# Masks by ScalarE and GpSimd, spatial weights in six pieces, and two pieces of work a unit later in a fused attention and MLP kernel

## The chip, the core and the metric

One core of a Trainium2 chip runs the whole program as one launch. The core has TensorE (PE; its weight loads are shown as PEld), VectorE (DVE), ScalarE (ACT), GpSimd (POOL), and SyncE (SP), which here issues every transfer. The metric is the device time of one execution in microseconds (us); smaller is better. Each engine works through its own list of instructions in order and waits at an instruction whose inputs or buffers aren't ready.

## The reference

Three stages for 4 batches of 768 tokens, the output of each being the input of the next.

```python
for t in range(S):                       # attention: 8 heads of 48, D = 48
    state = alpha[:, :, t, :, None] * state + einsum('bhd,bhe->bhde', k[:, :, t], v[:, :, t])
    y[:, :, t] = einsum('bhd,bhde->bhe', q[:, :, t], state)
x = y with the heads side by side        # 384 wide
xn = (x - mean) / sqrt(var + 1e-6) * g_ln
x = x + relu(xn @ w_ch1) @ w_ch2         # first MLP, 1536 wide
h = gelu(x @ w_in)                       # second MLP, 1024 wide
u, v = h[..., :512], h[..., 512:]
v_n = (v - mean) / sqrt(var + 1e-6) * g_ln
gated = u * (einsum('ts,bsd->btd', w_sg, v_n) + b_sg[None, :, None])   # mixes the 768 tokens of a batch
out = x + gated @ w_out
```

## The kernel before

**Precision.** Matmuls of the MLPs run in float16 with each operand split into a high half (rounded) and a low half (what rounding lost); three passes (high x high, low x high, high x low) make one product. So each weight and each intermediate result is followed by a ScalarE copy (high) and a subtraction (low) on VectorE or GpSimd. The helper `low` (L155) writes a low half on VectorE if its first argument is true, otherwise on GpSimd; `split2` (L151) does high and low with a scale, the low one on VectorE.

**Attention.** The 24 chunks of 128 tokens (6 a batch) each go through some 20 steps (`att_steps`): alpha is transposed, running products of it along the chunk (scans) give F and K, q and k are multiplied on, TensorE makes the scores of two sets of heads (tile sc in PSUM), the part above the diagonal is set to zero, and the masked scores times v plus q times the state give the output; its mean is taken off, its halves (xsp) are transposed by a transfer into xhT. For the first batch (chunks 0 to 5, `whole`) the scores stay float32 and `masked` makes the mask on VectorE in one instruction from PSUM (L499), by a product with the tile causal; for the later chunks masking goes other ways, which the change doesn't touch. From chunk 8 on, alpha, q and k are transposed by transfers instead of TensorE (L299, L302, L315). Input tiles inp are two; the load of chunk i + 2 waits for the last reading of chunk i (L565, `stats`).

**The MLPs.** Chunks go in 12 groups of two. For each group there are units of TensorE work: A (first product, L706, output hT by ScalarE L711 and VectorE L712), T (transposes of x), C (L787 gives v, then L816 gives u, both through gelu), B (second product, L740). For each batch there are six units D, the spatial mix (L837), and six units E, the output product (L866). In C, v is normalized: VectorE takes mean and variance (L792, L794), GpSimd makes the factor r2 in six instructions on single columns (`rms_scale`, L247 to L252), VectorE applies it (L799), and the halves vn follow (L802, `low`). This last part, `normalize`, is put off in the source: `finish` runs it while the next unit of C is written down. In D, VectorE scales the sum out of PSUM into one of two buffers tm (L843), GpSimd multiplies by u (L846), ScalarE writes the gate's high half (L847), GpSimd its low half (L848). Sums of TensorE rotate through three PSUM banks (tag g).

**Weights.** They are loaded, converted and split in pieces while the first batch runs, one step of `wstep` after the other; a step also issues the next load. Loads go into three tiles stage. The spatial weights w_sg (768 x 768) come in three pieces of two row blocks (`wg_piece`, L210); each row block is split into two halves wsp, of which there is one pair of buffers at a time (tag cv, shared with small scratch tiles), and each half is transposed by a transfer into wgs, which D reads.

**Order.** The kernel writes down units, attention steps, loads and weight steps in the order of due times that it works out by hand from the constants of L20 (`events`, L1011 on); the weight steps of the last kind are due from C3 = 60 at a distance of R3. The framework then places the instructions on each engine with a planner of its own, which estimates when each would be ready; what is written down first isn't always placed first. `tc.issue_after(x)` pins what is written inside it behind x on x's engine, in the order of issue alone.

## Time and profile before

| what | value |
|---|---|
| time, median of 3 runs | 695.94 us (693.63 to 696.15) |
| the profiled execution: its own time | 695.21 us |
| its span, first to last instruction | 693.4 us |
| mean granted TensorE clock | 0.978 of full speed |
| busy: PE, DVE, ACT, POOL | 640.0, 460.7, 376.4, 250.5 us |

A row's time is that of one profiled execution. The "chain that ended last" follows the work back from the last instruction, at each step to what it had waited for. Idle time of an engine costs nothing unless something later on the chain waits for it.

### The profile page before, as it was taken

Reading aid. Unit: us, or ns where it says so; the run is one execution under the profiler, and the core shown is the slowest. Engines: PE = TensorE matmul, PEld = TensorE weight load, DVE = VectorE, ACT = ScalarE, POOL = GpSimd, SP = SyncE. Lnnn points to the kernel's source line nnn. Section 1 sums busy time; section 2 is a strip of 40 time slices with the busy share of each in tenths; the row PEclk is TensorE's granted clock in tenths of the full one; section 3 lists DMA queues with packets and bytes.
Section 4 is the critical chain, followed back from the end, with each engine's and each line's share of the span. In section 5 each row is a group of like instructions: output and inputs, shape, how many; then the busy total and the mean of one; then the engine's idle time right before and its main releaser. Section 6 shows DMA issues by size and latency. Waiting matters only on the chain.

```text
span 693.4 us, 14269 instructions
## 1 busy us (share of the span) xinstructions
PE 640.0 (92%) x5622; PEld 487.4 (70%) x5622; DVE 460.7 (66%) x879; ACT 376.4 (54%) x643; POOL 250.5 (36%) x474
## 2 busy tenths in 40 slices
PE   5989798899999988999999989997989999999996
PEld 3677596676666875677686876675677887676783
DVE  7799977868655568667664669638966777333325
ACT  3765435487834576477844587646753733332230
POOL 4232220534423662342523770521415652302261
PEclk9999989999999998999999998999999999999999
DMA  9996889648824747764724638674523322110102
GB/s 226 280 243 183 252 169 182 102 81 122 115 29 71 104 62 125 142 111 91 107 50 60 103 67 170 104 115 76 89 44 68 76 26 58 28 19 12 36 1 74
DMA packets 228636, 70.63 MB, mean 102 GB/s; under 512 B 219472, under 2 KB 222544, under 8 KB 228560
## 3 DMA queue, kind: packets, MB, share of 16 engines
q1 hardware_dynamic: 228560, 69.63, 54.3%
q8 instruction: 46, 0.75, 0.5%
q14 instruction: 30, 0.25, 0.1%
HBM read 35.79 MB, written 4.72 MB: 58 GB/s over the span
## 4 chain that ended last, share of the span: by engine, by line
PE 51%; DVE 19%; DMA 12%; ACT 10%; issue 5%; POOL 2%; SPq 1%; ACTq 0%; DVEq 0%
PE pg L740 11%; PE pg L706 10%; PE pgs L837 10%; PE pgo L866 6%; PE pgu L816 4%; PE pgv L787 4%; ACT stage L315 3%; DMA xhT<-xsp 3%; DMA wgs<-wsp 3%; DMA stage<-stage 2%; DMA stage<-in_moe_w_ch_dram 2%; DVE st_in L565 2%; DVE F L362 2%; ACT stage L299 2%; DVE hT L712 2%
## 5 line engine op out<-in xcount | busy, mean ns | idle before, releaser
L706 PE MATMUL pg<-xhT,w1s 128*128 128x256 f16 (+1 forms) x1404 | 153.8, 270 | 14.6 <-DVE hT L712 12.5
L706 PEld LDWEIGHTS <-w1s 128*128 128x128 f16 x1404 | 131.1, 100 | 33.2 <-issue 16.1
L740 PE MATMUL pg<-w2s,hT 128*128 128x384 f16 x864 | 145.3, 326 | 0.4 <-DVE hT L712 0.4
L740 PEld LDWEIGHTS <-hT 128*128 128x128 f16 x864 | 83.6, 98 | 53.9 <-issue 0.6
L837 PE MATMUL pgs<-wgs,vn 128*128 128x256 f16 x864 | 96.0, 273 | 0.0
L837 PEld LDWEIGHTS <-vn 128*128 128x128 f16 x864 | 84.1, 98 | 10.3
L315 ACT ACTIVATE stage<-stage 128x1024 uint16<-128x1024 uint16 x48 | 64.2, 1350 | 9.3 <-DMA stage<-stage 9.2
L712 DVE SCALAR_TENSOR_TENSOR hT<-pg,hT 128x512 f16<-128x512 f32 (+1 forms) x74 | 48.7, 670 | 29.4 <-ACT hT L711 29.2
L299 ACT ACTIVATE stage<-inp 128x1024 uint16<-128x1024 uint16 x48 | 49.1, 1046 | 20.6 <-DVE K L362 10.6
L156 POOL TENSOR_TENSOR kh<-K,kh 128x512 f16<-128x512 f32 x17 | 21.6, 1268 | 105.5 <-ACT kh L469 105.5
L711 ACT ACTIVATE hT<-pg 128x512 f16<-128x512 f32 (+1 forms) x74 | 41.4, 575 | 31.2 <-PE pg L706 31.2
L816 PE MATMUL pgu<-x2T,wis 128*128 128x256 f16 x432 | 49.6, 273 | 3.2 <-ACT vg L790 1.4
L787 PE MATMUL pgv<-wis,x2T 128*128 128x512 f16 x216 | 49.2, 379 | 0.5 <-DVE hT L712 0.5
L816 PEld LDWEIGHTS <-wis 128*128 128x128 f16 x432 | 41.8, 98 | 9.9 <-issue 2.3
L866 PE MATMUL pgo<-wos,uT 128*128 128x384 f16 x288 | 48.3, 326 | 0.0
L156 POOL TENSOR_TENSOR qs<-F,qs 128x512 f16<-128x512 f32 x18 | 20.2, 1123 | 70.9 <-ACT qs L447 70.8
L866 PEld LDWEIGHTS <-uT 128*128 128x128 f16 x288 | 27.9, 98 | 17.8
L843 DVE SCALAR_TENSOR_TENSOR tm<-pgs,g2c,bbc 128x256 f32<-128x256 f32 x48 | 20.7, 474 | 28.2 <-PE pgs L837 22.9
L552 DVE SCALAR_TENSOR_TENSOR vs<-inp,vs 128x384 f16<-128x384 f32 x18 | 15.0, 833 | 32.9 <-ACT vs L550 32.9
L787 PEld LDWEIGHTS <-x2T 128*128 128x128 f16 x216 | 20.6, 98 | 22.9 <-issue 0.6
L247 POOL TENSOR_SCALAR ve<-mvv 128x1 f32<-128x1 f32 x24 | 5.6, 235 | 84.1 <-DVE mvv L794 83.0
L847 ACT ACTIVATE uT<-tm 128x512 f16<-128x512 f32 x24 | 15.0, 625 | 38.7 <-POOL tm L846 38.7
(184 smaller groups left out, 1108.8 us busy)
## 6 DMA issues: line engine op xcount, KB each, us to landing
stage<-in_moe_w_ch_dram SPq DMA_DIRECT2D x24, 384.0 KB, 5.3
inp<-in_alpha_dram SPq DMA_DIRECT2D x24, 192.0 KB, 4.6
inp<-in_q_dram SPq DMA_DIRECT2D x24, 192.0 KB, 3.4
inp<-in_k_dram SPq DMA_DIRECT2D x24, 192.0 KB, 4.1
inp<-in_v_dram SPq DMA_DIRECT2D x24, 192.0 KB, 4.5
out_dram<-x SPq DMA_DIRECT2D x24, 192.0 KB, 1.9
stage<-in_moe_w_in_dram SPq DMA_DIRECT2D x4, 768.0 KB, 4.7
stage<-in_moe_w_sg_dram SPq DMA_DIRECT2D x6, 384.0 KB, 4.2
```

Of the source, the lines that this page charges most:

```text
L156: (nc.vector if on_dve else nc.gpsimd).tensor_tensor(out=out, in0=in0, in1=in1, op=ALU.subtract)
L299: nc.scalar.activation(out=sp, in_=t[:, n].rearrange("p h d -> p (h d)").bitcast(U16) .rearrange("p (x w) -> p w x", w=2), func=AF.Copy)
L315: nc.scalar.activation(out=words[:, :, :, gap:], in_=tr, func=AF.Copy)
L706: nc.tensor.matmul(out=pg[:, f, :], lhsT=w1s[:, a, kk, ff * P:(ff + 1) * P], rhs=xhT[j][:, r, kk, o], start=(n_ == 0), stop=(n_ == 3 * KD ...
L711: nc.scalar.activation(out=hi, in_=src, func=AF.Relu)
L712: last_dve[0] = nc.vector.scalar_tensor_tensor(out=lo, in0=src, scalar=0.0, in1=hi, op0=ALU.max, op1=ALU.subtract)
L740: nc.tensor.matmul(out=box[s], lhsT=hidden(a, f, s), rhs=w2s[:, r, f, :], start=(f == 0 and a == 0 and r == 0), stop=(f == KF - 1 and r == 1))
L787: nc.tensor.matmul(out=pg, lhsT=x2T[j][:, a, kk, o], rhs=wis[:, r, kk, DG:DI], start=(n_ == 0), stop=(n_ == 3 * KD - 1))
L816: nc.tensor.matmul(out=pg[:, f, :], lhsT=wis[:, a, kk, ff * P:(ff + 1) * P], rhs=x2T[j][:, r, kk, 0:N], start=(n_ == 0), stop=(n_ == 3 * K ...
L837: nc.tensor.matmul(out=pg[:, f, :], lhsT=vn[b * NCH + s][:, a, d * P:(d + 1) * P], rhs=wgs[th][:, r, s, :], start=(n_ == 0), stop=(n_ == 3 ...
L843: nc.vector.scalar_tensor_tensor(out=tm[:, f, :], in0=pg[:, f, :], scalar=g2c[:, d:d + 1], in1=bbc[:, th * U:(th + 1) * U], op0=ALU.mult, ...
L866: nc.tensor.matmul(out=pg, lhsT=gt[key][:, d // 2, a, d % 2, o], rhs=wos[:, r, d, :], start=(d == 0 and a == 0 and r == 0), stop=(d == KG ...
```

## The change

Four edits and a constant.

- Masks of the first batch: ScalarE copies the scores out of PSUM with the scale, and GpSimd sets the part above the diagonal to zero in place (`affine_select`), instead of one VectorE instruction per set of heads; two sets for each of six chunks.
- Spatial weights: six pieces of one row block, each in a tile stage of its own, instead of three of two. ScalarE scales the block in place, ScalarE writes the high half, GpSimd subtracts for the low half. The distance R3 of the weight steps goes from 5 to 3, and the counts NW of steps that D and E need grow by three.
- Gate: high and low half (and, in the last batch, a square for a check) are written down a unit later, in the next unit of D, or in the next unit of A after a batch's last; `low` now puts every second low half on VectorE. `in_order` pins them behind the last instruction written on ScalarE, VectorE and GpSimd.
- v's normalization keeps its place in the source, but `in_order` pins it behind the last instruction written on ScalarE and VectorE.

```diff
--- before.py
+++ after.py
@@ -70,7 +70,7 @@
     NG3 = S // U
 
     NW = [KF // 2, KF, KF + DI // U]
-    NW += [NW[2] + NCH // 2, NW[2] + NCH // 2 + KG // 2]
+    NW += [NW[2] + NCH, NW[2] + NCH + KG // 2]
     NST = 3
     NF = NCH
 
@@ -208,18 +208,20 @@
     wo_piece = row_pieces(wos, w_out, S_WO, False)
 
     def wg_piece(i):
+
         if i == 0:
             wg_tiles()
-        t = stage_tile().bitcast(F32).rearrange("p (n s) -> p n s", n=2)
-        for n in range(2):
-            nc.sync.dma_start(out=t[:, n], in_=w_sg[(2 * i + n) * P:(2 * i + n + 1) * P, :])
+        t = stage_tile().bitcast(F32)[:, 0:S]
+        nc.sync.dma_start(out=t, in_=w_sg[i * P:(i + 1) * P, :])
 
         def split():
-            for n in range(2):
-                sp = [p2.tile([P, S], F16, tag="cv", name="wsp") for _ in range(2)]
-                split2(sp[0], sp[1], t[:, n], S_SG)
-                for a in range(2):
-                    nc.sync.dma_start_transpose(out=wgs[i][:, a, :, n * P:(n + 1) * P], in_=sp[a])
+            sp = [p2.tile([P, S], F16, tag="cv", name="wsp") for _ in range(2)]
+            nc.scalar.activation(out=t, in_=t, func=AF.Copy, scale=S_SG)
+            nc.scalar.activation(out=sp[0], in_=t, func=AF.Copy)
+            nc.gpsimd.tensor_tensor(out=sp[1], in0=t, in1=sp[0], op=ALU.subtract)
+            o = slice(i % 2 * P, i % 2 * P + P)
+            for a in range(2):
+                nc.sync.dma_start_transpose(out=wgs[i // 2][:, a, :, o], in_=sp[a])
         return split
 
     wgs = []
@@ -496,8 +498,9 @@
             if whole:
                 m = T[f"ss{e}"] = T[f"ss{e}"].rearrange("p a n t -> p (a n t)").bitcast(F32) \
                     .rearrange("p (n t) -> p n t", n=NP)
-                nc.vector.scalar_tensor_tensor(out=m, in0=T["sc", e], scalar=S_V, op0=ALU.mult, op1=ALU.mult,
-                                               in1=causal.unsqueeze(1).to_broadcast([P, NP, P]))
+                nc.scalar.activation(out=m, in_=T["sc", e], func=AF.Copy, scale=S_V)
+                nc.gpsimd.affine_select(out=m, in_=m, pattern=[[0, NP], [1, P]], compare_op=ALU.is_ge, fill=0.0,
+                                        base=0, channel_multiplier=-1)
                 return
             if chosen(MB):
                 m = T["sm", e] = T["sc", e]
@@ -678,6 +681,15 @@
     s_split = [None]
 
     last_dve = [None]
+
+    def in_order(work, *engines):
+
+        traced = nc.cur_bb.bb.instructions
+        with ExitStack() as behind:
+            for e in engines:
+                behind.enter_context(tc.issue_after(next(n for n in reversed(traced) if n.engine == e.engine)))
+            work()
+
     stats_step = {}
 
 
@@ -711,6 +723,7 @@
                     nc.scalar.activation(out=hi, in_=src, func=AF.Relu)
                     last_dve[0] = nc.vector.scalar_tensor_tensor(out=lo, in0=src, scalar=0.0, in1=hi, op0=ALU.max,
                                                                  op1=ALU.subtract)
+                    finish_gate()
                 units.append((unit, per * 9 * N / 2400.0, (2, 3, 5, 6)[((u + 1) * per - 1) // KD],
                               groups[j][0] * NCH + groups[j][1] + (part if j == 0 else 1)))
         return units
@@ -775,7 +788,7 @@
         def finish():
 
             if pending:
-                pending.pop()()
+                in_order(pending.pop(), nc.scalar, nc.vector)
 
         for s in range(n):
             i = b * NCH + c + s
@@ -822,6 +835,13 @@
             units.append((unit, per * 9 * N / 2400.0, NW[1] + KG // 2 + u + 1))
         return units
 
+    gate_pending = []
+
+    def finish_gate():
+
+        if gate_pending:
+            in_order(gate_pending.pop(0), nc.scalar, nc.vector, nc.gpsimd)
+
     def D_units(b):
         units = []
         for th in range(S // U):
@@ -844,12 +864,18 @@
                                                        in1=bbc[:, th * U:(th + 1) * U], op0=ALU.mult, op1=ALU.add)
                     o = slice(2 * dp, 2 * dp + 2)
                     nc.gpsimd.tensor_tensor(out=tm, in0=tm, in1=uT[key][:, o, :], op=ALU.mult)
-                    nc.scalar.activation(out=gt[key][:, dp, 0], in_=tm, func=AF.Copy)
-                    nc.gpsimd.tensor_tensor(out=gt[key][:, dp, 1], in0=tm, in1=gt[key][:, dp, 0], op=ALU.subtract)
-                    if b == B - 1:
-                        n_ = 2 * th + dp
-                        nc.scalar.activation(out=junk()[:, 0:512].rearrange("p (a b) -> p a b", a=2), in_=tm,
-                                             func=AF.Square, accum_out=st_g[:, n_:n_ + 1])
+                    finish_gate()
+
+                    def halves_of_gate():
+                        nc.scalar.activation(out=gt[key][:, dp, 0], in_=tm, func=AF.Copy)
+                        low(dp, gt[key][:, dp, 1], tm, gt[key][:, dp, 0])
+                        if b == B - 1:
+                            n_ = 2 * th + dp
+                            nc.scalar.activation(out=junk()[:, 0:512].rearrange("p (a b) -> p a b", a=2), in_=tm,
+                                                 func=AF.Square, accum_out=st_g[:, n_:n_ + 1])
+                    gate_pending.append(halves_of_gate)
+                    if b == B - 1 and th == S // U - 1 and dp == KG // 2 - 1:
+                        finish_gate()
                 units.append((unit, 36 * U / 2400.0, NW[3]))
         return units
 
@@ -940,7 +966,7 @@
                                     op0=ALU.mult)
         nc.vector.tensor_scalar(out=diags[0][:, KD], in0=ident, scalar1=S_W2, scalar2=None, op0=ALU.mult)
         pre = [(w1_piece, n) for n in range(KF // 2)] + [(w2_piece, n) for n in range(KF // 2)] \
-            + [(wi_piece, n) for n in (2, 3, 0, 1)] + [(wg_piece, n) for n in range(NCH // 2)] \
+            + [(wi_piece, n) for n in (2, 3, 0, 1)] + [(wg_piece, n) for n in range(NCH)] \
             + [(wo_piece, n) for n in range(KG // 2)]
         pre.reverse()
         ready = []
```

## Rows read from the trace of the kernel before

**Rows 1.** The page's fourth part: the chain of work that ended last, as shares of the span by engine.

```profile
PE 51%; DVE 19%; DMA 12%; ACT 10%; issue 5%; POOL 2%; SPq 1%; ACTq 0%; DVEq 0%
```

**Rows 2.** Busy time by stretch. Columns: start and end of the stretch, its length, busy time (and number of instructions) of PE, PEld, DVE, ACT and POOL, the granted TensorE clock, the transfers' share of the 16 DMA engines, and GB/s.

```profile
30.00:60.00 30.00, 27.20 (x324) 24.14 (x323) 27.02 (x47) 17.79 (x29) 9.98 (x19) 1.00 1.03 234
60.00:90.00 30.00, 24.50 (x188) 18.22 (x188) 28.66 (x50) 16.56 (x25) 5.42 (x14) 0.89 0.80 216
...
300.00:400.00 100.00, 99.50 (x925) 76.61 (x923) 62.76 (x116) 63.34 (x111) 45.66 (x80) 1.00 0.55 89
```

**Rows 3.** TensorE in order of time, around the first MLP of groups 0 and 1. Columns: start and duration in us, engine, line, operation, output and inputs, shapes, how many; in brackets the idle time of the engine just before and what ended it.

```profile
40.62 1.67 PE L706 MATMUL pg<-xhT,w1s 128*128 128x128 f16 x27 [1.02 <-DMA xhT<-xsp]
...
93.76 2.13 PE L706 MATMUL pg<-xhT,w1s 128*128 128x256 f16 x18
...
105.29 0.63 PE L460 MATMUL pk<-ident,K 128*128 128x128 f32 x4 [1.12 <-DVE K L320]
...
111.22 1.13 PE L577 MATMUL psd<-inp,ks 128*128 128x96 f32 x8 [1.45 <-ACT ks L461]
...
114.42 1.76 PE L604 MATMUL psy<-inp,ss 128*128 128x48 f32 x14 [0.55 <-DVE ss L499]
...
125.19 2.12 PE L816 MATMUL pgu<-x2T,wis 128*128 128x256 f16 x18 [0.76 <-DVE nmu L656]
```

**Rows 4.** VectorE (first five rows) and ScalarE (last row) in order of time, in the stretch of the masks and the spatial weights. Columns as in rows 3.

```profile
73.04 1.28 DVE L499 SCALAR_TENSOR_TENSOR wk<-sc,causal 128x512 f32<-128x512 f32 x2
...
87.41 0.61 DVE L659 SCALAR_TENSOR_TENSOR xsp<-psy,st_mv,xsp 128x384 f16<-128x384 f32 x1
...
99.59 0.96 DVE L153 SCALAR_TENSOR_TENSOR wsp<-stage,wsp 128x768 f16<-128x768 f32 x1 [3.13 <-DMA wgs<-wsp]
...
112.80 0.96 DVE L153 SCALAR_TENSOR_TENSOR wsp<-stage,wsp 128x768 f16<-128x768 f32 x1
...
122.58 0.96 DVE L153 SCALAR_TENSOR_TENSOR wsp<-stage,wsp 128x768 f16<-128x768 f32 x1 [0.73 <-DMA wgs<-wsp]
...
109.07 0.84 ACT L152 ACTIVATE wsp<-stage 128x768 f16<-128x768 f32 x1 [2.50 <-DMA wgs<-wsp]
```

**Rows 5.** The stretch of the gating units of batch 0 and what follows it, and one row of the same place in batch 1: TensorE (five rows), VectorE (four) and ScalarE (one), each in order of time. Columns as in rows 3.

```profile
221.85 4.09 PE L837 MATMUL pgs<-wgs,vn 128*128 128x256 f16 x36
...
249.88 6.06 PE L706 MATMUL pg<-xhT,w1s 128*128 128x256 f16 x54
...
259.48 0.24 PE L583 MATMUL psd<-vs,ks 128*128 128x96 f16 x2 [2.45 <-ACT vs L550]
...
263.79 6.46 PE L706 MATMUL pg<-xhT,w1s 128*128 128x256 f16 x41 [2.55 <-DVE hT L712]
...
416.98 7.21 PE L706 MATMUL pg<-xhT,w1s 128*128 128x256 f16 x46 [2.73 <-DVE hT L712]
...
237.82 0.86 DVE L843 SCALAR_TENSOR_TENSOR tm<-pgs,g2c,bbc 128x256 f32<-128x256 f32 x2
240.66 0.88 DVE L843 SCALAR_TENSOR_TENSOR tm<-pgs,g2c,bbc 128x256 f32<-128x256 f32 x2 [1.97 <-POOL uT L848]
...
244.76 2.23 DVE L362 TENSOR_TENSOR_SCAN K<-stage,reset 128x516 f32<-128x516 f32 x1
...
267.19 1.20 DVE L362 TENSOR_TENSOR_SCAN K<-stage,reset 128x516 f32<-128x516 f32 x1
...
245.94 0.63 ACT L847 ACTIVATE uT<-tm 128x512 f16<-128x512 f32 x1 [3.42 <-POOL tm L846]
```

**Rows 6.** Busy time by stretch, as in rows 2, around TensorE's wait at 263.79 us.

```profile
260.80:267.50 6.70, 4.15 (x25) 2.97 (x22) 6.70 (x11) 2.95 (x7) 1.31 (x4) 0.50 0.90 147
```

**Rows 7.** Groups of instructions of one line and shape over the whole span. Columns: line, engine, operation, output and inputs, shapes, how many; busy us and mean ns of one; idle time of the engine just before them and what ended it.

```profile
L846 POOL TENSOR_TENSOR tm<-tm,uT 128x512 f32<-128x512 f32 x24 | 32.3, 1348 | 10.3 <-DVE tm L843 10.0
...
L848 POOL TENSOR_TENSOR uT<-tm,uT 128x512 f16<-128x512 f32 x24 | 28.5, 1188 | 12.9 <-ACT uT L847 12.9
...
L156 DVE TENSOR_TENSOR ss<-sc,ss 128x512 f16<-128x512 f32 x36 | 24.0, 676 | 5.6 <-ACT ss L523 5.4
...
L156 POOL TENSOR_TENSOR vn<-vg,vn 128x512 f16<-128x512 f32 x19 | 23.3, 1226 | 14.5 <-ACT vn L802 14.3
...
L499 DVE SCALAR_TENSOR_TENSOR ss<-sc,causal 128x512 f32<-128x512 f32 x8 | 5.2, 682 | 0.0
...
L461 ACT ACTIVATE ks<-pk 128x512 f32<-128x512 f32 x4 | 2.4, 588 | 0.4 <-PE pk L460 0.4
...
L347 POOL MEMSET F<- 128x512 f32 x4 | 2.1, 526 | 13.5 <-PE sc L491 6.9 <-PE psy L598 6.6
```

**Rows 8.** GpSimd (two rows) and VectorE (one) in order of time. Columns as in rows 3.

```profile
43.86 1.70 POOL L252 TENSOR_TENSOR rx<-ra,rr 128x1 f32<-128x1 f32 x1
...
65.13 0.19 POOL L252 TENSOR_TENSOR rx<-ra,rr 128x1 f32<-128x1 f32 x1
...
57.84 1.58 DVE L153 SCALAR_TENSOR_TENSOR w2s<-stage,w2s 128x768 f16<-128x768 f32 x1
```

**Rows 9.** The last line of the view of the tile wsp (the halves of the spatial weights): the time of its transposes from issue to landing.

```profile
DMA to landing us min/median/max: 2.8/3.9/5.3
```

**Rows 10.** Who waited for whom, over the whole span. Columns: us in total, how many times, the longest.

```profile
DVE vg L799 <- POOL rv L252: 23.9, 14, 4.0
...
PE pg L706 <- DVE hT L712: 12.5, 7, 2.9
```

More of the change, by code (lines that the diff above doesn't have):

```diff
@@ L19 @@
 EPS = 1e-6
-LATE, TC, D0, DS, DX, KQ, NE, KA, LD, S0, A0, S1, A1, S2, A2, S3, A3, S4, A4, S5, A5, C0, R0, C1, R1, C2, R2, C3, R3, MB, MD, QB, HB, KV, KG_, KW, KW2 = 16.42, 19.13, 26, 0.88, 1.18, 8.0, 4.0, 8.0, 5.66, 0.8, 16, 8, 12, 22, 14, 30, 14, 40, 14, 48, 14, 2, 3, 20, 3, 34, 3, 60, 5, 224.0, 96.0, 0.0, 96.0, 19.0, 0.0, 10.0, 0.0
+LATE, TC, D0, DS, DX, KQ, NE, KA, LD, S0, A0, S1, A1, S2, A2, S3, A3, S4, A4, S5, A5, C0, R0, C1, R1, C2, R2, C3, R3, MB, MD, QB, HB, KV, KG_, KW, KW2 = 16.42, 19.13, 26, 0.88, 1.18, 8.0, 4.0, 8.0, 5.66, 0.8, 16, 8, 12, 22, 14, 30, 14, 40, 14, 48, 14, 2, 3, 20, 3, 34, 3, 60, 3, 224.0, 96.0, 0.0, 96.0, 19.0, 0.0, 10.0, 0.0
 NE = int(NE)
```

## The prediction

> **What bounds the kernel now.** I read the page's chain first, then the busy time by stretch, then each engine in order of time around the places where TensorE stood idle. TensorE holds only half of the chain that ended last; VectorE holds 19% and transfers 12% [rows 1]. By stretch the kernel has two parts [rows 2]. From 30 to 90 us VectorE is the full engine: 27.0 of 30 us and then 28.7 of 30, with ScalarE at 17 or so and GpSimd at 10 and 5. From 300 to 400 us TensorE is full (99.5 of 100) and VectorE is at 63. So an instruction taken off VectorE has a value before 90 us, and later only where a wait of TensorE can be followed back to it.
>
> The places where TensorE stands idle are few. The first MLP unit of group 0 starts at 40.62 us, after a wait for a transfer and not for VectorE; group 1 starts at 93.76 us [rows 3]. Its input is the transposed output of chunk 3, which VectorE writes only at 87.41 us [rows 4], in a stretch in which it hardly paused. So group 1 is late because VectorE is. Between 104 and 126 us come four short waits (1.12, 1.45, 0.55, 0.76 us) for K, for ks, for a mask and for a mean [rows 3]. From there on TensorE has a backlog. Its larger waits stand shortly after the gating units (D): 2.45 and 2.55 us after those of batch 0, 2.73 us after those of batch 1 [rows 5]. In the 6.7 us around the second of these the granted clock is 0.50, its lower level (1.2 GHz), after TensorE had stood idle [rows 6], and the stretch in batch 1 looks the same; 41 and 46 matmuls then take 6.46 and 7.21 us where 54 take 6.06, so the clock costs 6.46 - 41 x 0.112 = 1.9 us and 7.21 - 46 x 0.112 = 2.1 us [rows 5].
>
> **The masks of the first batch.** Twelve VectorE instructions of 0.68 us go, 8.2 us together [rows 7]. Twelve ScalarE copies from PSUM come; the nearest row is the copy of ks, same size and type, 0.59 us, so 7.1 us [rows 7]. ScalarE has 12 us free in each of the two 30 us stretches [rows 2] and hides them. Twelve GpSimd selects in place come, for which the trace has no row. A memset of the same size (no input) takes 0.53 us, the gate's product of that size (two inputs) 1.35 us [rows 7]; a select has one input, so I take 0.8 us, 9.6 us in all, with ends at 6.4 and 16.2. What of the 8.2 us lies on the path? Chunks 0 and 1 don't count, since group 0 waits for a transfer. The pairs of chunks 2 and 3 (the second at 73.04 us) stand in the full stretch ahead of 87.41: a pair shows 1.28 us, of which the last bit overlaps the next instruction [rows 4], so I count 1.2 us each, 2.4 us.
>
> Against that stands a price that GpSimd's rows show. GpSimd's r2 took 1.70 us at 43.86 and 0.19 us at 65.13, the first while VectorE ran splits and conversions that read two SBUF tensors; and at 57.84 a split of VectorE took 1.58 us while GpSimd's state product ran [rows 8], where one of that size takes 0.96 [rows 4]. Each engine held the other up, by 0.6 us on VectorE's side. The Trainium skill, "GPSIMD Engine Reference", section "Key points", says that GpSimd shares its SBUF interfaces with VectorE and contends with VectorE instructions that have two SBUF inputs or run in a two-port mode; the trace agrees (1.58 against 0.96 us), and by that rule alone each select could cost VectorE as much as it saves, so that the masks would give nothing. By the rows, two of the four selects meeting such an instruction for the 0.53 us of a memset cost 1.0 us; all four for 1.23 us (GpSimd's subtraction) cost 4.9. I take 1.0, because about half of VectorE's instructions in that stretch read PSUM or one tensor. Masks: -2.4 + 1.0 = -1.4 us, between -2.4 and +2.5.
>
> **The spatial weights.** VectorE loses six subtractions of 0.96 us, 5.8 us, and the standing still before them for the transposes that free the two halves' buffers, 3.13 us at the worst [rows 4]. ScalarE gains six passes in place like its present 0.84 us [rows 4], 5.0 us. GpSimd gains six subtractions of 768 elements: the 512-element one takes 1.23 us, so 1.84 each, 11 us [rows 7]. Per piece the way from landing to transpose grows by 1.84 - 0.96 = 0.9 us and by a ScalarE pass that needs no free buffer and can run early. Six pieces end perhaps 6 us after today's last at 122.58 us [rows 4]; the first gating matmul is at 221.85 [rows 5], so the length itself is hidden. On the transfer queue there are six loads of half the size and the same twelve transposes. What VectorE's standing still costs TensorE are the waits at 105.29 (K's product, behind the subtraction at 99.59), 114.42 (the mask behind the one at 112.80) and 125.19 (the mean behind the one at 122.58) [rows 3, 4]: 1.12 + 0.55 + 0.76 = 2.4 us. The 1.45 us at 111.22 stay, since ScalarE's high half still waits for the buffers as it does today (2.50 us at 109.07) [rows 4]. I take -2.4, between -3.9 (that one too) and what GpSimd's queue may cost, which is a rival below.
>
> **v's normalization.** VectorE stood 23.9 us, 14 times, for r2 from GpSimd [rows 10]. All that TensorE lost behind VectorE's low half hT is 12.5 us in seven waits [rows 10], of which 5.3 are the two after D; the other 7.2 bound what this edit can give. A pin changes nothing where the planner already had this order, and behind such a stand VectorE mostly had time to spare, TensorE having 99.5 of 100 us of work. I take -0.5, between -7.2 and 0.
>
> **The gate's halves.** Of 24 subtractions on GpSimd (1.19 us) 12 go to VectorE, where the one of equal size takes 0.68 us: 14.3 us less there, 8.1 us more here [rows 7]. In the gating stretch of batch 0 VectorE waited 1.97 us at 240.66 for the buffer tm, which GpSimd's subtraction held; ScalarE waited 3.42 us at 245.94 behind the gate's copy; the second scan then took 2.23 us while GpSimd worked [rows 5]. The scan of the next chunk, of the same size, took 1.20 us with GpSimd idle [rows 5]; I count half of the 1.0 us between them as won, 0.5. The edit takes away the 1.97 us and those 0.5, and adds 0.68 us for the low half. It also holds tm for a unit longer: where VectorE catches up on two units in a row (the second at 237.82 us), the second must wait until GpSimd has done a product and a subtraction after the first, 1.35 + 1.19 us, and so starts some 2 us later, the third about 0.9 us later than now. So 1.97 + 0.5 - 0.68 - 0.9 = 0.9 us a batch, 1.8 for the two batches after which TensorE waits. Ends: -11.7 (the three waits, 7.7 us, and 4.0 us of lower clock) and +8.1 (every low half on the path).
>
> **Sum.** -1.4 - 2.4 - 0.5 - 1.8 = -6.1 us. The profiled execution took 695.2 us, 1.8 more than its span; that leaves 689.1. It lies 0.7 us under the median of the runs, so I predict 690.0 us for the median. About 3.5 us (0.5%) is what a measurement of this kernel can tell from no change: below 692.5 counts as faster.
>
> **Rivals.** *The ports and the ring take it back (0.30).* The selects cost VectorE 2.4 us and the longer hold of tm cancels what the gate gives; then only 2.4 + 0.5 remain, 693.0 us, up to 696 if the weights give nothing. For it: the 1.70 and 1.58 us [rows 8], and a TensorE without idle time in most of the second part. Against it: GpSimd is idle in three quarters of the time from 30 to 90 us.
>
> *GpSimd's queue becomes the bound (0.20), slower.* GpSimd serves in order. A low half of the spatial weights that waits for its buffer stands for up to 3.9 us (median landing of a transpose [rows 9]) and then works 1.84 us. The masks of chunks 4 and 5 fall in just that time; a select queued behind such an instruction holds the score product of its chunk on TensorE for up to 5.7 us. Twice is 11.4 us, which against the 6.1 gives +5.3, 701 us; at one such wait the forecast's gain is gone, at two the kernel is slower. For it: VectorE and ScalarE stood 3.13 and 2.50 us at that spot. Against: TensorE has other work planned between scores and products.
>
> *The waits behind the gating units vanish (0.08).* If ScalarE, no longer held at 245.94, brings the next chunk forward by its 3.4 us, most of the 11.7 us goes: 690.0 + 1.8 - 11.7 = 680 us; half of it 685.
>
> **The numbers.** Forecast 0.42, with its own range 686 to 692.4. Faster is that and the last rival, 0.50; same 0.30; slower 0.20. From 681 to 700 leaves out half of the slower rival and a part of the fastest, under 2 in 10.
>
> **What would show it.** Right: group 1's first MLP matmul at about 92 us in place of 93.76; VectorE under 27 us in 60 to 90; no VectorE wait for the transposes of the spatial weights; no VectorE wait of 1.97 us for GpSimd in D; selects near 0.8 us. Wrong: long waits of TensorE for a select or a ks between 95 and 125 us; VectorE's splits at 1.3 us and more; waits of VectorE for tm in D as long as before, and those of TensorE after D grown. What would make the prediction wrong altogether is the planner: any edit lets it place other instructions differently, on every engine.

## The result and the profile after

The changed kernel takes 698.14 us (median; 695.61 to 702.64) against 694.85 (692.68 to 696.75) for the kernel before in the same runs: a ratio of 1.0057, 95% interval 1.0046 to 1.0069. It is slower by 3.3 us by the medians and 4.0 us by the ratio, where a gain of 6 us (690.0) was forecast. The time lies within the range of 681 to 700, but the direction was wrong: it is that of the rival that had 0.20. The profiled execution has a span of 695.8 us (before 693.4) and an own time of 697.64.

The page of the changed kernel, the chain that ended last:
```profile
PE 43%; DVE 21%; DMA 13%; ACT 10%; issue 6%; POOL 5%; SPq 1%; ACTq 0%; DVEq 0%; POOLq 0%
```
TensorE's share fell from 51%, and GpSimd's rose from 2 to 5% [rows 1]. Busy time by stretch (columns: stretch, us, then busy us and instructions of PE, PEld, DVE, ACT, POOL, then granted clock, DMA share, GB/s):
```profile
30.00:60.00 30.00, 27.93 (x341) 25.24 (x340) 25.69 (x44) 19.49 (x33) 14.48 (x25) 1.00 1.08 247
60.00:90.00 30.00, 21.72 (x165) 16.17 (x163) 25.76 (x46) 18.55 (x30) 10.48 (x16) 0.94 0.78 183
```
VectorE did get its room: it was busy for 25.76 us of the 30 us before 90 us, where it had 28.66 [rows 2]. TensorE in order of time around group 1 (start, length, what ended the idle time before):
```profile
87.75 1.99 PE L601 MATMUL psy<-state,F 128*128 128x96 f32 x8 [2.06 <-ACT x L667]
89.54 3.19 PE L718 MATMUL pg<-xhT,w1s 128*128 128x256 f16 x14
...
114.79 0.42 PE L607 MATMUL psy<-inp,ss 128*128 128x48 f32 x2 [2.81 <-POOL ss L502]
```
Group 1 starts at 89.54, 4.2 us earlier than in [rows 3] and earlier than the "about 92" of the forecast, but its first matmuls run at half pace (14 in 3.19 us, where [rows 3] have 18 in 2.13). And the 2.81 us for a select are new. GpSimd in that place:
```profile
112.46 1.64 POOL L221 TENSOR_TENSOR wsp<-stage,wsp 128x768 f16<-128x768 f32 x1 [5.08 <-DMA wgs<-wsp]
114.04 0.10 POOL L352 MEMSET K<- 128x4 f32 x1
114.10 1.23 POOL L502 TENSOR_SCALAR_AFFINE_SELECT ss<-ss 128x512 f32<-128x512 f32 x2
```
The select stands behind a low half of the spatial weights that waited for its buffer, as one rival had it. After this wait the granted clock was 0.88 from 114 to 118 us and 0.69 from 118 to 122. VectorE in the gating stretch of batch 0, and TensorE behind it:
```profile
240.63 0.88 DVE L863 SCALAR_TENSOR_TENSOR tm<-pgs,g2c,bbc 128x256 f32<-128x256 f32 x2 [2.50 <-POOL uT L156]
241.43 0.68 DVE L156 TENSOR_TENSOR uT<-tm,uT 128x512 f16<-128x512 f32 x1
...
244.20 1.40 DVE L364 TENSOR_TENSOR_SCAN F<-stage,reset 128x516 f32<-128x516 f32 x1
245.52 2.12 DVE L364 TENSOR_TENSOR_SCAN K<-stage,reset 128x516 f32<-128x516 f32 x1
```
```profile
259.91 0.24 PE L586 MATMUL psd<-vs,ks 128*128 128x96 f16 x2 [2.91 <-ACT vs L553]
260.90 0.96 PE L586 MATMUL psd<-vs,ks 128*128 128x96 f16 x10 [0.75 <-DVE vs L555]
264.21 5.98 PE L718 MATMUL pg<-xhT,w1s 128*128 128x256 f16 x40 [2.35 <-DVE hT L724]
```
The wait for tm is 2.50 us where it was 1.97, one scan is faster (1.40 against 2.19), and TensorE's waits after the gate are as long as before [rows 5].

A unit that starts early says little when the planner has put other work behind it. So I worked out from the traces when each kernel had done the same amount of TensorE work: each fp16 matmul counts its columns at 2.4 GHz, each fp32 one 0.0725 us, in the order in which they ran. Each row is one amount of work: the time by which before had done it, then how much later (+) or earlier (-) the others had.
```
work    before   after  masks weights  gate   norm  split-now  masks+split-now
 50      95.18   +0.20  +1.70  -0.57  -1.03  +0.36   +0.56    +1.06
 62     111.74   -1.92  -0.34   -2.09  -1.29  +0.01   +0.31    -0.59
 65     116.56   +0.41  -0.41  -2.45  -1.05  +0.37   +0.71    -1.21
 70     121.76   +2.09  -0.29   -2.45  -1.05  +0.37   +0.71    -1.09
 75     127.97   +1.33  -1.21  +3.68  -1.06  +0.77   +0.86    -2.01
 90     147.07   +2.27  -2.73  +3.79  -1.16  +0.67   +0.76    -3.55
190     256.42   -0.03  -2.26  +2.37  -1.51  +0.67   +0.78    -2.77
200     274.76   +0.20  -2.02  +2.72  -1.52  +0.81   -2.39    -6.06
260     337.65   +1.89  -2.14  +2.62  +0.45  +0.74   -1.18    -4.86
340     426.20   +2.34  -2.18  +2.07  +0.78  +0.64   -2.57    -6.26
450     547.92   +2.98  -2.34  +2.79  +1.35  +0.72   -3.57    -6.61
585     687.02   +2.29  -2.34  +2.79  +0.65  +0.71   -2.93    -5.99
```
The columns beside "after" belong to the experiments below: four single edits, the gate's split with nothing deferred (split-now), and the masks with it. Each column is one execution; against the medians of many runs they are off by up to 2 us.

At 95 us, with group 1 started 4.2 us early, the changed kernel had done no more work than the kernel before. Between the rows 62 and 70, which hold the wait for the select and the lower clock after it, it goes from 1.92 us ahead to 2.09 behind, 4.0 us. In most of the single edits what is lost or won by 150 us stays to the end. In the changed kernel it does not: at 256 us it is level with the kernel before, and the 2.3 us by which it ends later are lost after that, 1.7 of them between the rows 200 and 260, where the gate edit alone loses 2.0.

### The profile page after: what moved, and what is told of

It reads as the page before. It is cut to its first block, busy times and chain, and to the rows that moved or that the text cites. A ratio compares the mean times of both kernels' runs of the same rounds, so it can differ in the third digit from the quotient of the medians.

```text
span 695.8 us, 14294 instructions
## 1 busy us (share of the span) xinstructions
PE 641.8 (92%) x5622; PEld 487.8 (70%) x5622; DVE 454.8 (65%) x873; ACT 385.8 (55%) x661; POOL 262.9 (38%) x480
## 4 chain that ended last, share of the span: by engine, by line
PE 43%; DVE 21%; DMA 13%; ACT 10%; issue 6%; POOL 5%; SPq 1%; ACTq 0%; DVEq 0%; POOLq 0%
PE pg L753 9%; PE pg L718 8%; PE pgo L892 6%; PE pgs L857 6%; PE pgv L800 4%; PE pgu L829 4%; DMA stage<-stage 3%; ACT stage L317 3%; DVE st_in L568 2%; DVE F L364 2%; ACT stage L301 2%; DMA stage<-in_moe_w_ch_dram 2%; DVE K L364 2%; DMA wgs<-wsp 2%; DVE sc L507 2%
## 5 line engine op out<-in xcount | busy, mean ns | idle before, releaser
L866 POOL TENSOR_TENSOR tm<-tm,uT 128x512 f32<-128x512 f32 x24 | 32.3, 1349 | 25.7 <-DVE tm L863 25.7
```

Source lines behind the costliest of these rows:

```text
L866: nc.gpsimd.tensor_tensor(out=tm, in0=tm, in1=uT[key][:, o, :], op=ALU.mult)
```

## The experiments

**Each edit alone** on the kernel before (the diffs are the parts of the change). A result is the ratio to the kernel before in the same runs, with its 95% interval; differences in us are worked out from the ratio.

> The masks of the first batch alone on ScalarE and GpSimd, all else as before. Theory A (GpSimd's queue): the masks do no harm by themselves, the low halves of the spatial weights in front of them do; so no wait of TensorE over 1 us for a select between 95 and 125 us, and a time of -2 to 0 us against before. Theory B (the shared port takes it back): selects of 0.6 us hold VectorE's splits up, 0 to +1 us. Theory C (planner): any shift of up to 3 us, with its cause in stretches after 150 us that the edit doesn't touch.

Measured: 0.9947 (0.9922 to 0.9972), -3.7 us.

> The spatial weights alone in six pieces with the low half on GpSimd and R3 of 3. Theory A: with the masks on VectorE nothing of TensorE queues behind these low halves, so the 2.8 us wait of the changed kernel at 114.8 us is absent and the time is -2 to +0.5 us. Theory L (loads): a piece takes a whole tile stage, so its load starts late and ScalarE, which scales it in place, stands for it (9.6 us in the changed kernel); then the first MLP of group 1 still takes over 27 us from its start to the first v unit (23.8 before) and the time is +1 to +3 us.

Measured: 1.0062 (1.0041 to 1.0082), +4.3 us.

> The gate's halves a unit later, every second low half on VectorE, alone. Theory R (ring): tm is held a unit longer, VectorE waits more for it (11.2 us in the changed kernel, 5.3 before), and the 2.3 us that the changed kernel loses after 250 us appear here: +1.5 to +3 us, from the first E unit of batch 0 on. My prediction's own step says -1.8 us. Theory C (planner) says that the losses stand elsewhere and the time is within 1 us.

Measured: 1.0038 (1.0023 to 1.0052), +2.6 us.

> v's normalization pinned, alone. If the pin had removed VectorE's stand for r2, VectorE's 23.9 us would be below 10 us and the time -0.5 to -3 us. The changed kernel shows 26.1 us, so I expect that the planner had this order nearly everywhere: 24 us again, and a time within 0.7 us; a loss of 1 us or more would make this pin a part of the loss after 250 us, because the halves of v then stand behind gelu and attention work on ScalarE.

Measured: 0.9997 (0.998 to 1.0015). VectorE still stands 24.1 us for r2.

The product of the four is 1.0044, the measured 1.0057: the effects add within their intervals. So the sign does not come from a clash between these four; some combinations further down do not add. The masks pay more than forecast, weights and gate cost.

**The full change without the weights edit.**

> The full change without its weights edit, so the masks, the gate and the normalization. If the effects add: 0.9947 x 1.0038 x 0.9997 = 0.9982, and against the full change's 1.0057 the weights edit costs 0.75% in its company, more than the 0.62% it costs alone, because the select's wait of 2.81 us at 114.8 us is then gone. If the gate's cost depends on the planner's placement after 260 us and not on the edit, the masks' gain shows whole: 0.994 to 0.996.

Measured: 0.9983 (0.9966 to 0.9999), as the sum has it. Beside the other edits the weights edit costs 0.74% (1.0057 to 0.9983).

**Masks of chunks 4 and 5 alone.**
```diff
+                if i < 4:
+                    nc.vector.scalar_tensor_tensor(out=m, in0=T["sc", e], ...
+                    return
                 nc.scalar.activation(out=m, in_=T["sc", e], func=AF.Copy, scale=S_V)
```


> The masks edit for chunks 4 and 5 alone (four of its twelve masks); chunks 0 to 3 keep VectorE's product. Theory C, the reason of the prediction: the gain comes from VectorE's full stretch ahead of 87 us, so from chunks 2 and 3, and this run gives 0.999 to 1.001. Theory D: the gain of the masks (0.9947 alone) is that of TensorE's waits between 104 and 126 us, in which chunks 4 and 5 are masked, and VectorE works off its queue there: 0.995 to 0.997, with the waits of 1.12, 1.45 and 0.55 us shorter by 2 us or more together. Between them: both stretches carry a part.

Measured: 0.998 (0.9966 to 0.9993). A third of the masks, which the forecast did not count, brings -1.4 of the -3.7 us. By the traces its share is larger: its profiled execution ends 2.28 us ahead of the kernel before, that of all twelve masks 2.34 (table). That the other chunks carry the rest stands on the two ratios alone, and their intervals touch.

**The weights: why they cost.** The edit alone, TensorE (in order of time) and then the stretches as above:
```profile
123.26 3.65 PE L818 MATMUL pgu<-x2T,wis 128*128 128x256 f16 x18 [3.18 <-DVE hT L714]
128.13 2.12 PE L818 MATMUL pgu<-x2T,wis 128*128 128x256 f16 x18 [1.22 <-ACT vg L792]
130.84 3.41 PE L742 MATMUL pg<-w2s,hT 128*128 128x384 f16 x20 [0.59 <-ACT vg L792]
```
```profile
114.00:122.00 8.00, 6.08 (x38) 3.63 (x36) 5.15 (x15) 2.84 (x4) 1.14 (x2) 1.00 0.85 165
122.00:126.00 4.00, 2.74 (x14) 1.94 (x14) 1.48 (x4) 1.92 (x3) 3.59 (x7) 0.63 0.39 90
```
The kernel before, same stretches:
```profile
114.00:122.00 8.00, 7.58 (x52) 5.35 (x53) 5.93 (x14) 5.46 (x7) 0.00 (x0) 1.00 0.76 160
122.00:126.00 4.00, 3.24 (x31) 2.77 (x30) 3.42 (x8) 1.56 (x3) 1.17 (x4) 1.00 0.82 118
```
By row 65 (at 114 us here) TensorE was 2.45 us ahead: group 1 had started 0.34 us earlier (93.42), the 1.45 us for ks [rows 3] were gone, and the waits for K and for the mask were 0.91 and 0.17 us in place of 1.12 and 0.55. Then TensorE ran dry (no matmul had its inputs) for 3.18 us, and the granted clock was 0.63 from 122 to 126 us: 14 matmuls, 31 before. Between the rows 65 and 75 of the table 6.1 us are lost. ScalarE and GpSimd of this kernel in that place:
```profile
119.43 1.07 ACT L135 ACTIVATE bits<-stage 128x768 uint16<-128x768 uint16 x1 [3.31 <-DMA stage<-in_moe_w_out_dram]
120.37 0.57 ACT L713 ACTIVATE hT<-pg 128x512 f16<-128x512 f32 x1
124.08 0.84 ACT L220 ACTIVATE wsp<-stage 128x768 f16<-128x768 f32 x1 [3.13 <-POOL wsp L221]
...
127.48 0.60 ACT L792 ACTIVATE vg<-pgv 128x512 f32<-128x512 f32 x1
```
```profile
121.62 2.42 POOL L221 TENSOR_TENSOR wsp<-stage,wsp 128x768 f16<-128x768 f32 x1 [6.86 <-DMA wgs<-wsp]
```
Two suspects: the low half on GpSimd (late, 2.42 us, the next high half waits for it), and six pieces in the ring of stage tiles (the load of w_out then lands late). First the low half back on VectorE:
```diff
-            nc.gpsimd.tensor_tensor(out=sp[1], in0=t, in1=sp[0], op=ALU.subtract)
+            nc.vector.tensor_tensor(out=sp[1], in0=t, in1=sp[0], op=ALU.subtract)
```


> The weights edit alone, with one thing back as it was: the six low halves of the spatial weights are subtracted on VectorE (0.96 us each in the kernel before) and not on GpSimd (2.4 us in the run of this edit alone). Six loads, six pieces, the scaling in place on ScalarE and the earlier output weights stay. Theory A, the length of the low half on GpSimd is the cost (a piece's two buffers are held until it is done, ScalarE's next high half waits for them, and the gelu of group 0's gating input stands behind that high half): the ratio to before is 0.996 to 1.001, group 1's second MLP layer starts no later than 127.5 us, and TensorE's waits of 3.18 and 1.22 us at 123 and 128 us are gone. Theory B, six pieces instead of three in the same ring of three stage tiles hold the loads up: the ratio stays 1.004 to 1.007 and the waits stay.

Measured: 1.0025 (1.0011 to 1.004). Then three pieces as before, with the new split of a row:
```diff
-                split2(sp[0], sp[1], t[:, n], S_SG)
+                nc.scalar.activation(out=t[:, n], in_=t[:, n], func=AF.Copy, scale=S_SG)
+                nc.scalar.activation(out=sp[0], in_=t[:, n], func=AF.Copy)
+                nc.gpsimd.tensor_tensor(out=sp[1], in0=t[:, n], in1=sp[0], op=ALU.subtract)
```


> The kernel before with its three pieces of two rows each and its loads and their order as they were; only the split of a row is changed: ScalarE scales in place, ScalarE takes the high half, GpSimd subtracts the low half. Theory A (the low half on GpSimd is the cost): 1.003 to 1.008, with TensorE waits of 2 us or more between 118 and 132 us that lead back to a high half waiting for GpSimd. Theory B (six pieces are the cost): 0.996 to 1.000, because VectorE loses six subtractions and its standing still (3.13 us at the worst) and nothing else changes.

Measured: 0.9988 (0.9975 to 1.0001). Neither theory held alone: six pieces cost 0.25% even with VectorE's low half, and GpSimd's low half costs 0.37% more among six pieces and nothing among three (beside the masks it is otherwise, see the end of this part). In the run of three pieces TensorE ran dry as well, and so it was in all of these runs:
```profile
123.11 6.88 PE L818 MATMUL pgu<-x2T,wis 128*128 128x256 f16 x36 [3.30 <-DVE hT L714]
```
```profile
122.00:126.00 4.00, 2.90 (x14) 2.07 (x14) 3.19 (x7) 3.29 (x6) 3.23 (x7) 0.50 0.49 95
```
Here 36 matmuls take 6.88 us at a clock of 0.50. They took 5.01 in the kernel before, with a wait in between. By the work done, 2.66 us ahead at 114 us became 2.66 us behind at 131; later stretches gave 3.6 us back.

Then the pace of the pieces (R3 back from 3 to 5), which puts the last high half behind the gelus:

> The weights edit alone with the pace of the pieces as in the kernel before (a piece every 5 units of the plan, not every 3; nothing else). In ScalarE's order the sixth piece's high half then stands behind the two gelus of group 0's gating input, not ahead of them. Theory A', refined after the two runs on the weights (what costs is that ScalarE's order has the last high half, which waits for GpSimd and for a transpose, ahead of the first gelu: that gelu starts at 120.66 us in the kernel before and at 123.7, 126.0 and 127.5 us in the three weight kernels, which gave 0.9988, 1.0025 and 1.0062): the first gelu starts before 124 us and the ratio is 0.996 to 1.000. Theory B (six loads and six pieces in the stage ring): 1.003 to 1.007 as with the faster pace.

Measured: 1.0066 (1.0047 to 1.0086). The sixth high half is not the cause: it no longer stands ahead of the gelus, and the ratio is no better. But the run did not bring the gelus forward as theory A' wanted. The first one in the kernel before, and then the first in this run, with TensorE's waits for both gelus:
```profile
120.66 0.60 ACT L790 ACTIVATE vg<-pgv 128x512 f32<-128x512 f32 x1
```
```profile
125.23 0.60 ACT L792 ACTIVATE vg<-pgv 128x512 f32<-128x512 f32 x1
```
```profile
125.88 2.13 PE L818 MATMUL pgu<-x2T,wis 128*128 128x256 f16 x18 [0.52 <-ACT vg L792]
130.28 3.90 PE L742 MATMUL pg<-w2s,hT 128*128 128x384 f16 x23 [2.27 <-ACT vg L792]
```
Other work held ScalarE up: w_out's first load came to it at 119.41 (3.19 us waited), as against 116.15 before (0.98), and for the second it waited 2.52 us, ahead of the second gelu. So that late gelus cost is not refuted. TensorE's dry stretch was 3.06 us here, up to 123.24. Last, four buffers:
```diff
-            sp = [p2.tile([P, S], F16, tag="cv", name="wsp") for _ in range(2)]
+            sp = [p2.tile([P, S], F16, tag=g, name="wsp") for g in ("cv", "tm")]
```


> The weights edit alone (1.0062), whose pieces get four half buffers in place of two: the low half lies in the buffers that the gate uses from 222 us on. Theory T (a piece's high half waits on ScalarE until the transposes of the piece before have left the two buffers; group 1's last high half hT stands behind it, TensorE runs out of work at 120 us, stands over 3 us and its clock falls to the lower level): no ScalarE wait of 2 us or more for a transpose between 100 and 125 us, TensorE's wait at 123 us under 1 us, the granted clock 1.00 from 118 to 130 us, and a ratio of 0.994 to 0.998. Theory B (six loads of one row in the stage ring and on the transfer queue): the loads' waits on ScalarE (2.0 and 2.6 us) stay, TensorE's wait at 123 us stays over 2 us, 1.002 to 1.006.

Measured: 1.0022 (1.0007 to 1.0037). ScalarE and then TensorE:
```profile
114.88 1.07 ACT L135 ACTIVATE bits<-stage 128x768 uint16<-128x768 uint16 x1 [5.08 <-DMA stage<-in_moe_w_out_dram]
```
```profile
124.89 5.64 PE L818 MATMUL pgu<-x2T,wis 128*128 128x256 f16 x36 [3.06 <-DVE hT L714]
```
The wait and the ratio are those of theory B: the buffers account for 0.4% of the edit's 0.62%. The rest, and the wait of 3 us, stay with six pieces; ScalarE then stands 5.08 us for w_out, and VectorE's low half hT stands behind w_out's integer passes.

The five runs side by side, as in the table above, with the time at which the second load of w_out was issued (two lines of it as SyncE shows them, the kernel before and the weights edit):
```
work    before  weights  low half on  three   slower   four
                 edit     VectorE     pieces   pace   buffers
 70     121.76  -2.45     -2.33       -2.66   -2.49    -0.85
 75     127.97  +3.68     +2.42       +2.66   +3.13    +3.21
 90     147.07  +3.79     +1.49       -0.95   +4.14    +0.41
585     687.02  +2.79     +0.41       -2.06   +4.55    +0.83
issued  111.70  124.07    121.43      109.35  124.06   111.80
ratio           1.0062    1.0025      0.9988  1.0066   1.0022
```
```profile
111.70 0.82 SPq L193 DMA_DIRECT2D stage<-in_moe_w_out_dram  x2
```
```profile
124.07 0.81 SPq L193 DMA_DIRECT2D stage<-in_moe_w_out_dram  x2
```
All five lose 4.1 to 6.1 us between the rows 70 and 75, three pieces too, which are not slower than the kernel before. So the dry stretch alone is not the price. What tells the five apart is whether TensorE wins the time back by row 90: three pieces and four buffers do, and the two slowest, in which TensorE goes on to wait for the gelus, do not. These two are also those in which w_out's second load is issued last. The traces show why it is late: in the weights edit w_out's two loads are issued at 114.79 and 124.07, each 0.03 us after GpSimd has ended a low half (113.12 + 1.64 and 121.62 + 2.42), which frees a tile of the ring, and in the run with the low half on VectorE at 113.52 and 121.43, each 0.02 us after VectorE has. The first load then comes to ScalarE ahead of hT, the second between the two gelus. So the pieces do hold the loads up. That this is all that six pieces cost is argued from the order of the five runs, not shown.

**The gate: deferral and split apart.** The deferral with all low halves on GpSimd (`low(False, ...)` in the new code):

> The gate edit alone without its split: the two halves are deferred by a unit as in the change, but all low halves stay on GpSimd. Theory E, the deferral is the cost (a buffer tm is held a unit longer, and VectorE waits for it): 1.003 to 1.007, with waits of VectorE for GpSimd at tm of 5 us or more together for batch 0. Theory F, the price is a collision that the reordering moves (a VectorE scan at twice its time beside a GpSimd subtraction, which stands in the group after the gate, at 296 and 440 us, and TensorE's waits of 0.5 and 0.9 us at 321 and 330 us follow): the ratio is within 0.998 to 1.003 if the scans there take 1.2 us, and as in the full gate edit (1.004) if they take 2 us.

Measured: 1.0051 (1.0034 to 1.0068). VectorE's waits for tm in batch 0:
```profile
240.94 0.88 DVE L859 SCALAR_TENSOR_TENSOR tm<-pgs,g2c,bbc 128x256 f32<-128x256 f32 x2 [2.49 <-POOL uT L156]
244.38 0.88 DVE L859 SCALAR_TENSOR_TENSOR tm<-pgs,g2c,bbc 128x256 f32<-128x256 f32 x2 [2.56 <-POOL uT L156]
...
256.70 0.88 DVE L859 SCALAR_TENSOR_TENSOR tm<-pgs,g2c,bbc 128x256 f32<-128x256 f32 x2 [2.97 <-POOL uT L156]
```
8.0 us, where [rows 5] have 1.97. The last of them reaches TensorE:
```profile
257.63 2.13 PE L714 MATMUL pg<-xhT,w1s 128*128 128x256 f16 x18 [1.92 <-DVE tm L859]
```
Both scans of the next group take 1.2 us in this run (at 291 and 292 us), so theory F, a moved collision, does not explain its loss; the longer hold of tm does. And the split at once:
```diff
-                    nc.gpsimd.tensor_tensor(out=gt[key][:, dp, 1], in0=tm, in1=gt[key][:, dp, 0], op=ALU.subtract)
+                    low(dp, gt[key][:, dp, 1], tm, gt[key][:, dp, 0])
```


> The gate's other half of the edit: every second low half is subtracted on VectorE, at once, with nothing deferred. Theory E (the deferral costs, the split pays): 0.997 to 0.9995, since the deferral alone gave 1.0051 and both together 1.0038; VectorE's waits for the buffer tm in the gating stretch of batch 0 sum to 2 us or less where the deferral had 8.0, and both scans of the stretch are near 1.2 to 1.4 us. Theory F' (VectorE's extra 0.68 us a low half stand on the path as much as the split frees): 1.000 to 1.002.

Measured: 0.993 (0.991 to 0.995), -4.9 us. VectorE and TensorE:
```profile
240.20 1.17 DVE L156 TENSOR_TENSOR uT<-tm,uT 128x512 f16<-128x512 f32 x1 [0.73 <-ACT uT L847]
241.47 0.88 DVE L843 SCALAR_TENSOR_TENSOR tm<-pgs,g2c,bbc 128x256 f32<-128x256 f32 x2
...
243.46 1.57 DVE L362 TENSOR_TENSOR_SCAN F<-stage,reset 128x516 f32<-128x516 f32 x1
244.95 1.20 DVE L362 TENSOR_TENSOR_SCAN K<-stage,reset 128x516 f32<-128x516 f32 x1
```
```profile
261.57 7.71 PE L706 MATMUL pg<-xhT,w1s 128*128 128x256 f16 x54 [3.15 <-DVE hT L712]
```
VectorE no longer waits for GpSimd at tm in this stretch, both scans are shorter (2.77 us together, 4.42 before), and of TensorE's three waits (2.45, 0.75 and 2.55 us) one is left: 3.2 us are won between the rows 190 and 200 of the table. That the scans matter is suggested by the gate edit's own run, which lost 2 us between the rows 200 and 260. VectorE, GpSimd and TensorE there:
```profile
295.84 2.12 DVE L362 TENSOR_TENSOR_SCAN K<-stage,reset 128x516 f32<-128x516 f32 x1
```
```profile
294.96 1.91 POOL L156 TENSOR_TENSOR vn<-vg,vn 128x512 f16<-128x512 f32 x1 [1.94 <-ACT vn L811]
```
```profile
321.34 4.04 PE L796 MATMUL pgv<-wis,x2T 128*128 128x512 f16 x18 [0.52 <-DVE hT L720]
329.64 2.12 PE L825 MATMUL pgu<-x2T,wis 128*128 128x256 f16 x18 [0.87 <-ACT vg L799]
```
In the kernel before GpSimd's subtraction came later, and the scan was:
```profile
295.69 1.21 DVE L362 TENSOR_TENSOR_SCAN K<-stage,reset 128x516 f32<-128x516 f32 x1
```
The planner moved the collision out of the gate into the next group. The split alone has one there too (1.87 us for the other scan) and loses 1.2 us. The gate edit's profiled execution ends only 0.65 us later than that of the kernel before; where the rest of its 2.6 us falls is not shown.

**In the full change, the halves formed at once, the split kept.**

> The full change with one thing undone: the gate's halves are formed at once, not a unit later; every second low half stays on VectorE. Theory E (the deferral takes away what the split gives): 1.0057 x 0.993 / 1.0038 = 0.995, TensorE's waits after each gating stretch near 3 us in all rather than 6. Theory P (where the planner puts things after any edit decides, and the single runs were luck): 1.000 to 1.006.

Measured: 0.9972 (0.9958 to 0.9986). Theory E has the direction and TensorE's wait after the gate (3.20 us left); its 0.995 is a little more than was gained. In the full change the deferral makes 0.85% (1.0057 to 0.9972), more than the whole loss. The wait for a select stays in this run:
```profile
113.99 0.66 PE L607 MATMUL psy<-inp,ss 128*128 128x48 f32 x2 [2.60 <-POOL ss L502]
```

**What pays, together.**

> Two parts of the change that pay alone, on the kernel before: the masks on ScalarE and GpSimd, and the gate's split without the deferral. If the effects add: 0.9947 x 0.993 = 0.988, 686 us. If not (Theory P: placement decides): 0.992 to 0.998.

Measured: 0.9919 (0.9897 to 0.994), 689.10 us: the best kernel, though 0.4% short of the sum, which is about as much as the three intervals allow.

> As the run before with the weights edit in six pieces and four half buffers on top. If theory T holds and the effects add: 0.983 to 0.988. If the six pieces cost by their loads, or a select behind a low half on GpSimd holds TensorE near 114 us: 0.989 to 0.996.

Measured: 0.9963 (0.9944 to 0.9982). That is 0.44% above the run before. Its TensorE waits 2.56 us up to 123.18, now for a mean on VectorE. Six pieces cost here as well, though w_out's second load is issued at 111.37, as early as in the run before (111.41): a late second load is not the reason here.

> The masks, the gate's split without the deferral, and three pieces of two rows whose low halves go to GpSimd. If the split of the weights adds its 0.9988 to the 0.9919 of the other two: 0.989 to 0.992. If a select of chunks 4 and 5 stands behind a low half of the weights on GpSimd, TensorE waits 2 us or more for a select near 114 us, and its clock falls: 0.994 to 0.999.

Measured: 0.9946 (0.993 to 0.9962). The time is that of the second theory, but not its reason: there is no wait for a select, and the clock is 1.00 up to 138 us. Waits of 1.36, 0.72, 1.06 and 2.01 us between 110 and 142 us, for hT, x, K and a half of the scores, take their place.

A run of the masks with these three pieces alone gave 1.0011 (0.9992 to 1.003), where 0.9935 was expected if the effects add and 0.996 to 1.000 if a select stands behind a low half. It has no trace that can be compared with the others. So the new split of three pieces, harmless by itself, takes back the whole gain of the masks, and 0.27% where the gate's split is there as well; why is open.

## Why the prediction was wrong, by its own steps

**Masks** (-1.4; measured -3.7). Right in direction, mis-sized, and not by the path that was given. The term counted 2.4 us ahead of 87.41 us, which would bring group 1 forward. With the masks alone group 1 did start 2.95 us earlier (90.81), yet TensorE's work was 1.7 us behind at 95 us (row 50). It goes to 2.73 ahead by 147 us, in the stretch of chunks 4 and 5, which the term left out (-1.4 us by themselves). So the start of group 1, named as the sign of being right, was a poor one, and that it came true is no proof of the path.

A select took 0.64 us where nothing disturbed it (two in 1.22), not 0.8. The port price was there, but smaller than the 1.0 us. With the masks alone five of the twelve selects took 0.77 to 1.34 us, and three VectorE instructions beside selects took 1.27 to 1.31 us in place of 0.95. GpSimd and VectorE at chunk 2:
```profile
49.53 1.06 POOL L500 TENSOR_SCALAR_AFFINE_SELECT ss<-ss 128x512 f32<-128x512 f32 x1
50.58 1.31 POOL L500 TENSOR_SCALAR_AFFINE_SELECT ss<-ss 128x512 f32<-128x512 f32 x1
```
```profile
50.13 1.27 DVE L139 SCALAR_TENSOR_TENSOR stage<-stage 128x768 int32<-128x768 int32 x1
```
VectorE's pass L139, which reads two SBUF tensors, took 0.93 to 0.96 us all 18 times in the kernel before. The price to VectorE is 0.3 us for chunks 2 and 3 and 1.0 us for all twelve masks. The rule of the Trainium skill ("GPSIMD Engine Reference", section "Key points") agrees with these selects and with the scan that took 2.12 us beside a subtraction; that the masks might give nothing by it did not come true.

**Weights** (-2.4; measured +4.3). What failed is the sentence "so the length itself is hidden", because the first gating matmul comes at 221.85. The pieces have a nearer deadline than their consumer: what stands behind them in the orders of ScalarE, GpSimd and VectorE (hT of group 1, w_out's pieces, the gelus). TensorE reached that point earlier, found nothing ready, and stood for 3 us in one piece; the clock fell after it, an effect that the prediction priced after the gate and nowhere else. In the edit alone the time was not won back afterwards, and TensorE's next waits were for the gelus. That TensorE was 2.45 us ahead at 114 us, as much as the 2.4 that were counted, is luck: the largest part is the 1.45 us for ks, which the prediction said would stay, 0.91 of the 1.12 us for K stayed, and the 0.76 us at 125.19 come only after that point.

**Normalization** (-0.5; measured -0.2, between -1.4 and +1.0): the reason given, that a pin changes nothing where the order is the same, fits: VectorE's stand for r2 is 24.1 us after the pin and was 23.9 [rows 10].

**Gate** (-1.8; measured +2.6). Two terms mis-sized with opposite sign. The split was worth far more than 0.5 - 0.68 + 1.97: -4.9 us, because every second low half on VectorE frees GpSimd, and so tm and the scans. The longer hold of tm was priced at 0.9 us a batch; by itself it made 8.0 us of waits, and with the split still 2.50, more than the 1.97 it was to remove. What failed is the price of the hold: in the full change it takes back what the split gives, 0.85%.

**The rivals.** "GpSimd's queue becomes the bound" had the sign and a place that exists (2.81 us at 114.79). In the changed kernel this is where the weights edit takes its time from TensorE: 4.0 us between the rows 62 and 70, at one wait where the rival had two; without the weights edit the full change is 1.37 us ahead at row 70. But the loss does not need it: without any select on GpSimd the weights edit costs 0.62%, against 0.74% in company, by the dry stretch, which ends 8.5 us later. Nor does it decide the sign: the full change with the halves at once keeps such a wait (2.60 us at 113.99) and is faster than the kernel before. "The ports and the ring take it back" named the ring rightly, as no more than a gain cancelled; the ports cost a little. "The waits behind the gating units vanish" came true in part for the split without the deferral, which leaves one wait of three; with the deferral all three stay.

## What to carry to other kernels

A preparatory chain is hidden only if what is queued behind its instructions, on every engine that it uses, has time as well; look for the next instruction behind it, not for its consumer. Deferring the release of a buffer with two copies made the producer wait 2.5 to 3 us each time it caught up: shorten the holder first, as here by moving half of the subtractions. When judging a reordered schedule, compare the work done by a given time and not the start of a named unit.

## What was not expected of the hardware

In the 4 us from 122 to 126 us, which hold the end of a stand of 3.18 or 3.30 us, TensorE's granted clock was 0.63 and 0.50. But it is not always so: in the run with the slower pace it stood 3.06 us in the same place and the clock stayed at 1.00, with 20 matmuls in the same 4 us:
```profile
122.00:126.00 4.00, 2.24 (x20) 1.86 (x20) 3.21 (x6) 3.41 (x5) 3.76 (x5) 1.00 0.39 85
```
The length of the stand alone does not tell the two apart, since with four buffers it was 3.06 us as well and the clock was 0.74 from 126 to 130 us; what does wasn't tried. A scan of VectorE goes from 1.2 to 2.1 us beside a GpSimd subtraction. A select in place does less: it goes from 0.64 to as much as 1.34 us beside a VectorE pass over two SBUF tensors, and that pass from 0.95 to 1.28.
